# Turning the intermediate spectrum with VectorE in 32x32 squares instead of TensorE transposes, in a long-convolution kernel

## The chip, the cores and the metric

The kernel runs on one core of a Trainium2 chip. A core has five engines, each with its own queue of instructions that it works off in order: TensorE (PE in the profile, with its weight loads shown apart as PEld), VectorE (DVE), ScalarE (ACT), GpSimd (POOL) and SyncE (SP), which here does nothing but issue DMA transfers. They meet only at semaphores. TensorE writes its results to PSUM, eight banks of 128 partitions by 512 float32, from which VectorE and ScalarE copy them to SBUF. The metric is the device time of one execution in microseconds (us). A span runs from the first to the last instruction of the profiled execution.

## The reference

For a sequence u of 2048 steps by 512 channels:

```python
xn = layernorm(x)                                    # over the 512 channels
K[d, l] = Re(sum_n C[d,n] * dt*B[d,n] * exp(dt*A[d,n]*l))   # 128 complex modes
s = irfft(rfft(xn, 4096) * rfft(K, 4096))[:2048] + xn * Dskip   # causal convolution per channel
g = silu(gelu(xn @ w1 + b1) @ w2 + b2)               # 512 -> 1792 -> 512
return x + s * g
```

All is float32. The part that is changed is the way back of the convolution (the inverse transform), the product with g, and the sum with x.

## The kernel before

The program has two stages. The first, up to about 394 us of the trace, makes g (the two matrix products, each operand split in a high and a low part), the kernels K, and the normalised input; g goes to DRAM scratch tiles `gd`, K to `kgd`. The second stage, about which all of this document is, does the convolution. The two overlap for about 12 us.

**Blocks.** The convolution works in four blocks `b` of 128 channels. The 2048 steps are split as 32 by 64 (`N1 = 32`, `N2 = 64`), and the long transform is done as two short ones, both as matrix products with constant tables: `first_dft` over 32 (F below) and `second_dft` over 64 (S). The way back has a transform over 64 (`back_dft`, B), a turn that brings the other axis into the partitions (`swing`, w) and a transform over 32 (`last_dft`, L). F is done for u and for K, in two halves of channels each: four groups `(u, h)` a block, one block ahead.

**Slots.** S is cut into eight slots `g` of a block (`slot(b, g)`, L1020; main loop L1122). The program is written in the order in which each engine is to work it off, without a planner in this stage. Each slot begins with S on TensorE (L883: 32 small products with 64-row, 64-column tiles, each of them two instructions). ScalarE copies half of the result to SBUF (`spectrum`, tile `uh`, L891), and VectorE forms the two products with it (`product`, L900). After two slots `combine` (L909 to L912) makes the real and imaginary parts from sums and differences of these, in four instructions on 64 partitions, into the tile `Y`. Its rows 0 to 63 hold the real, 64 to 127 the imaginary parts.

Even slots also hold an F group for block b+1 (`first_dft`, L864; the results are copied by ScalarE, `first_out`, L870). Odd slots hold a B (`back_dft`, L918: two calls of four 128x128 products with the constant table `tcn`; `back_out`, L930, copies each call's bank into `Z`). The turn of block b-1 is in slots 3 and 5 (`swings`): 32 TensorE transposes (L936) of 128x128, each four copied out by ScalarE into tiles `bs` (`swing_out`, L944). The last transform of b-1 (`last_dft`, L975) is in slots 5 and 7: 64-row, 32-column tiles with the table `gc`, 512 columns. `last_out` multiplies the result with g on VectorE (L982) and adds x on GpSimd (L983); `store` (L992) sends it out.

**Loads and stores of the end.** For each block b-1, g and x come in four quarters (`tail_load`, L961 and L964, in slots 0, 1, 2 and 5, six transfers each), and the results leave in 16 transfers, all on SP's queue. Tiles `gb` and `xb` have three buffers each.

**PSUM.** Four of the eight banks belong to S (`ri`: two buffers of two banks). The other four serve F, B, w and L in turn (`bank`, L803: two pools, "c" and "a", of two buffers each, taken alternately). F takes all four, since its four channel groups run side by side; a call of B takes one.

**The last block** has no F. Its slots take the turn of block 2 in slots 2 to 5 and half of L of block 2 in slot 4; the other half follows after the slots. Then comes the end (L1125 to L1144): the last B, four dummy transposes (L1135), the turn in four quarters, L, products, sums and stores. Its loads go through GpSimd's queue in slots 1 to 4. Two of its quarters are done in another form (`rows_out`, L1006 to L1014), with a second table `gc2`.

Of the kernel before, what the change touches and what calls it, by code (L numbers as in the profile page):

```python
# [11 lines left out]
F32 = mybir.dt.float32  # L12
# [8 lines left out]
P = 128  # L21
L, D, NS, F = 2048, 512, 128, 1792
G = D // P
# [107 lines left out]
def _shape_constants():  # L131
# [4 lines left out]
    cg = np.zeros((2, N1, 2, 3, N1))  # L136
    for hh in range(2):
        for c, v in enumerate((np.cos(a).T, -np.sin(a).T)):
            cg[hh, :, c, 0] = v
            cg[hh, :, c, 1:].reshape(N1, N1, 2)[:, :, hh] = v  # L140
    cg = cg.reshape(P, 3 * N1)
# [14 lines left out]
    ct = ct.reshape(P, N1, 2, 2, 2, 16).transpose(0, 1, 4, 5, 3, 2)  # L156
# [16 lines left out]
def kernel(  # L173
# [7 lines left out]
    x_t = u[0].rearrange("(n h j t a q) d -> t h a j n q d", n=N1, h=2, j=2, t=2, a=2)  # L181
    o_l = out[0].rearrange("(r j q) d -> j r q d", j=2, q=NQ)
    o_t = out[0].rearrange("(n h j t a q) d -> t h a j n q d", n=N1, h=2, j=2, t=2, a=2)
    x_l = u[0].rearrange("(r j q) d -> j r q d", j=2, q=NQ)

# [5 lines left out]
    gd = [dram.tile([P, NQ * P], F32, name=f"gd{b}") for b in range(NB)]  # L191
# [251 lines left out]
    def z_store(t):  # L443
        zi = fin[t]
        for b in range(NB):
            (GP if t == NTB - 1 else SY).dma_start(gd[b].rearrange("p (q m) -> p q m", m=P)[:, t * TB:(t + 1) * TB, :], zi[:, :, b * P:(b + 1) * P])
# [341 lines left out]
    def open_mid():  # L788
        SB["pm"] = pm = opened(p2, "pm", "right")
        SB["ps"] = opened(pz, "psm", "left", bufs=2, space=PSUM)  # L790
        SB["tcn"] = pm.tile([P, N1, P], F32, name="tcn")
        SB["gc"] = pm.tile([P, N1], F32, name="gc")
# [109 lines left out]
    def combine(b, j, c, eng, js=slice(0, 4)):  # L902
        t, w = sm[b, j]
        if (b, j) not in yy:
            yy[b, j] = SB["pm"].tile([P, 4, 2, P], F32, tag="Y", name=f"Y_{b}_{j}", bufs=2)
        Y = yy[b, j].rearrange("p j a (r x) -> p a r j x", r=2)
        for ka in range(2):
            r = slice(ka * 64, ka * 64 + 64)
            if c == 0:  # L909
                eng.tensor_sub(Y[0:64, ka, :, js], t[r, 0, :, js], w[r, 1, :, js])  # L910
            else:
                eng.tensor_add(Y[64:128, ka, :, js], t[r, 1, :, js], w[r, 0, :, js])  # L912

    def back_dft(b, j, h):
        Y = yy[b, j].rearrange("p j a m -> p (j a) m")
        p = bank(f"sa{b}_{j}_{h}")
        for e in range(4):
            PE.matmul(p[:, e, :], Y[:, 4 * h + e, :], SB["tcn"][:, 8 * j + 4 * h + e, :], start=True, stop=True)  # L918
        yy[b, j, h] = p

    def back_out(b, j, h, engs=(A,)):
        if (b, "Z") not in yy:
            yy[b, "Z"] = SB["pm"].tile([P, 32, 2, N1, 2], F32, tag="Z", name=f"Z{b}", bufs=2)
        k = 8 * j + 4 * h
        src = yy.pop((b, j, h)).rearrange("p k (x h c) -> p x h k c", h=2, c=2)
        dst = yy[b, "Z"][:, :, :, k:k + 4, :]
        w = 4 // len(engs)
        for i, eng in enumerate(engs):
            n = slice(w * i, w * i + w)
            eng.copy(dst[:, :, :, n], src[:, :, :, n]) if eng is A else eng.tensor_copy(dst[:, :, :, n], src[:, :, :, n])  # L930

    def swing(b, q4, jj, wide=None):
        Z = yy[b, "Z"].rearrange("p (j r t q) h k c -> p j r t q (h k c)", j=2, r=2, t=2)
        p = bank(f"w{b}_{q4}_{jj}") if wide is None else wide[:, jj]
        for e in range(4):
            PE.transpose(p[:, e, :], Z[:, jj, q4 // 2, q4 % 2, e, :], ident)  # L936
        yy[b, q4, jj] = p

    def swing_out(b, q4, jj, eng):
        if jj == 0:  # L940
            yy[b, q4, "s"] = SB["pm"].tile([P, 2, 4, P], F32, tag="bs", name=f"bs{b}_{q4}", bufs=3)
        dst = yy[b, q4, "s"][:, jj].rearrange("p e (x r) -> p e r x", r=2)
        src = yy.pop((b, q4, jj)).rearrange("p e (r x) -> p e r x", r=2)
        A.copy(dst, src) if eng is A else V.tensor_copy(dst, src)  # L944

    gx = {}
    gc2 = dsk.rearrange("p b d -> p (b d)")[:, :2 * N1]

    def tail_load(b, i, q=SY, rows=False):
        cs = slice(b * P, (b + 1) * P)  # L950
        t = gx.pop((b, i, "t"), None) or new_tail(b, i)
        gx[b, i] = t
        if rows:
            n = slice(4 * i, 4 * i + 4)
            q.dma_start(t[0], gd[b].rearrange("p (q m) -> p q m", m=P)[:, n])
            for j in range(2):
                q.dma_start(t[1][j * 64:(j + 1) * 64], x_l[j, :, n, cs])
            return
        for a in range(2):
            r = slice(a * 64, (a + 1) * 64)  # L960
            q.dma_start(t[0][r], gd[b].rearrange("(j n h) (t a q m) -> t h a j n q m", n=N1, h=2, t=2, a=2, m=P)[i // 2, i % 2, a])  # L961
            for j in range(2):
# [212 lines left out]
```

## Time and profile before

| | |
|---|---|
| Three timed runs | 560.02, 560.35 (median), 561.1 us |
| Span of the profiled execution | 558.0 us |
| Around the span (start and end of the execution), median less span | 2.35 us |
| TensorE clock granted, mean | 0.998 |
| First S of block 0, 1, 2, 3 starts at | 405.9, 436.5, 473.1, 509.6 us |
| Last S ends | about 536.6 us |
| VectorE, last sum of the last block begins | 552.62 us |

The time of the profiled execution itself is not listed apart from the three; its span is what the rows below belong to. A row of the groups (by line) has the line, engine, operation, output and inputs with shapes, the count, then the busy time, the mean of one in ns, the idle time of the engine before them and what ended it. A row of the chain of waits or of the timeline has the start in us, the length in us, the engine and the line, with the number of instructions behind the x.

### The profile page before, as it was taken

How to read it: one execution, taken by the hardware profiler on the slowest of the kernel's cores; microseconds unless marked ns; L12 is line 12 of the kernel's file. 1: busy time of each engine (PE TensorE's matmuls, PEld its weight loads, DVE VectorE, ACT ScalarE, POOL GpSimd, SP SyncE). 2: the span in 40 equal slices, each digit the busy share in tenths (PEclk: the TensorE clock that was granted, in tenths of full speed). 3: DMA queues.
4: the chain of work that ended last, by engine and by line, in shares of the span. 5: the costliest groups of instructions: out<-in, count | busy, mean ns of one | idle time of the engine just before them, and what ended most of it. 6: DMA issues, size and time to landing. Idle time of an engine off the chain costs nothing.

```text
span 558.0 us, 17143 instructions
## 1 busy us (share of the span) xinstructions
PE 540.2 (97%) x7179; PEld 432.1 (77%) x7179; DVE 454.2 (81%) x697; ACT 407.8 (73%) x602; POOL 296.3 (53%) x403
## 2 busy tenths in 40 slices
PE   8899999999999999999999999999999999999995
PEld 7567777777777777767777777777889998988872
DVE  6899999999997799988988969877357657767874
ACT  3589997977598999668989798995355565564542
POOL 5639585776966769857718747540320305014323
PEclk9999999999999999999999999999999999999999
DMA  8959337267468392426167049205965583615945
GB/s 188 288 161 311 84 96 210 61 210 228 135 189 269 133 295 81 143 75 192 57 188 219 21 114 186 61 11 181 365 245 79 140 128 95 191 46 127 197 120 113
DMA packets 108345, 86.92 MB, mean 156 GB/s; under 512 B 44294, under 2 KB 87562, under 8 KB 108268
## 3 DMA queue, kind: packets, MB, share of 16 engines
q1 hardware_dynamic: 97584, 65.37, 43.8%
q0 software_dynamic: 9568, 19.93, 12.1%
q8 instruction: 56, 0.92, 0.7%
q10 hardware_dynamic: 1116, 0.53, 0.4%
q14 instruction: 21, 0.17, 0.1%
HBM read 52.25 MB, written 33.55 MB: 154 GB/s over the span
## 4 chain that ended last, share of the span: by engine, by line
PE 68%; DVE 16%; issue 6%; DMA 5%; SPq 2%; ACT 1%; POOL 1%; DVEq 0%; POOLq 0%
PE z L295 8%; PE z L296 7%; PE z L297 7%; PE f L256 7%; PE f L258 7%; PE f L257 7%; PE s L883 6%; PE kg L656 5%; PE s L864 4%; PE sa L918 3%; DMA w2s<-in_B_w_dram 2%; PE ph L595 2%; PE w L936 2%; DVE e L641 2%; DVE hl L282 2%
## 5 line engine op out<-in xcount | busy, mean ns | idle before, releaser
L618 POOL TENSOR_TENSOR mm<-mm,rc 128x32 f32<-128x32 f32 (+4 forms) x150 | 110.7, 738 | 11.8
L295 PE MATMUL z<-w2h,hh 128*128 128x512 f32 x224 | 97.9, 437 | 0.0
L256 PE MATMUL f<-xh,w1h 128*128 128x512 f32 x220 | 92.0, 418 | 0.5 <-ACT hf L270 0.5
L297 PE MATMUL z<-w2h,hl 128*128 128x512 f32 x224 | 88.5, 395 | 0.9 <-DVE hl L282 0.9
L296 PE MATMUL z<-w2l,hh 128*128 128x512 f32 x224 | 88.7, 396 | 0.0
L258 PE MATMUL f<-xh,w1l 128*128 128x512 f32 x220 | 86.9, 395 | 1.5 <-DVE w1l L241 1.5
L257 PE MATMUL f<-xl,w1h 128*128 128x512 f32 x220 | 86.7, 394 | 0.0
L883 PE MATMUL s<-X,mc 64*64 64x128 f32 x2048 | 63.5, 272 | 0.9 <-issue 0.9
L900 DVE TENSOR_TENSOR t<-s,uh 128x512 f32<-128x512 f32 x64 | 41.1, 685 | 25.9 <-ACT uh L891 25.6
L883 PEld LDWEIGHTS s<-X,mc 64*64 64x64 f32 x2048 | 56.0, 133 | 4.8 <-issue 2.7
L641 DVE TENSOR_TENSOR e<-mm,ra 128x1024 f32<-128x1024 f32 x32 | 47.8, 1495 | 4.7 <-POOL mm L618 3.2
L297 PEld LDWEIGHTS z<-w2h,hl 128*128 128x128 f32 x224 | 42.1, 188 | 11.7 <-DVE hl L282 1.8
L258 PEld LDWEIGHTS f<-xh,w1l 128*128 128x128 f32 x220 | 41.3, 188 | 11.9 <-DVE w1l L241 2.1
L615 POOL COPY mm<-rc 128x32 f32<-128x32 f32 x30 | 15.4, 512 | 65.4 <-DVE e L648 49.0
L256 PEld LDWEIGHTS f<-xh,w1h 128*128 128x128 f32 x220 | 41.5, 189 | 10.3 <-ACT hf L270 1.2
L282 DVE TENSOR_TENSOR hl<-hf,hh 128x512 fp32r<-128x512 f32 x56 | 46.7, 838 | 3.4 <-ACT hh L276 3.3
L295 PEld LDWEIGHTS z<-w2h,hh 128*128 128x128 f32 x224 | 42.5, 190 | 9.0
L609 DVE SCALAR_TENSOR_TENSOR ra<-ra,ph 128x512 f32<-128x512 f32 x64 | 43.6, 681 | 6.9 <-ACT ra L603 6.0
L296 PEld LDWEIGHTS z<-w2l,hh 128*128 128x128 f32 x224 | 42.3, 189 | 7.9
L257 PEld LDWEIGHTS f<-xl,w1h 128*128 128x128 f32 x220 | 41.4, 188 | 8.9
L870 ACT COPY X<-s 128x512 f32<-128x512 f32 x56 | 28.9, 598 | 25.6 <-PE s L864 25.6
L645 DVE TENSOR_TENSOR e<-mm,ra 128x1024 f32<-128x1024 f32 x32 | 45.6, 1425 | 0.0
(185 smaller groups left out, 1146.2 us busy)
## 6 DMA issues: line engine op xcount, KB each, us to landing
x<-in_A_u_dram SPq DMA_DIRECT2D x16, 256.0 KB
xs<-x SPq DMA_DIRECT2D x16, 256.0 KB
xt_h<-xh POOLq DMA_DIRECT2D x4, 1024.0 KB, 5.4
xt_l<-xl POOLq DMA_DIRECT2D x4, 1024.0 KB, 7.3
kgd<-ko SPq DMA_DIRECT2D x32, 128.0 KB
za<-zo SPq DMA_DIRECT2D x4, 1024.0 KB
xh<-xt_h POOLq DMA_DIRECT2D x4, 1024.0 KB, 6.8
xl<-xt_l POOLq DMA_DIRECT2D x4, 1024.0 KB, 10.1
```

What stands on the lines that cost most here:

```text
L256: PE.matmul(p, wh[:, k, :], xh[:, k, :], start=(k == 0), stop=False)
L257: PE.matmul(p, wh[:, k, :], xl[:, k, :], start=False, stop=False)
L258: PE.matmul(p, wl[:, k, :], xh[:, k, :], start=False, stop=(k == KD - 1))
L282: V.tensor_sub(hl, hf, hh)
L295: PE.matmul(z, hh[:, s], wh, start=(f0 == 0 and not rows), stop=False)
L296: PE.matmul(z, hh[:, s], wl, start=False, stop=False)
L297: PE.matmul(z, hl[:, s], wh, start=False, stop=(f0 == FA - 1))
L609: V.scalar_tensor_tensor(ra[:, 0, c], ra[:, 1, c], MAGIC, p, op0=ALU.subtract, op1=ALU.subtract)
L618: GP.tensor_mul(mv[:, :, 0:3:2, w:2 * w], mv[:, :, 0:3:2, 0:w], rc[:, 2 + 2 * i:4 + 2 * i, :].rearrange("p j c -> p c j").unsqueeze(3).to_ ...
L641: V.tensor_mul(e1, m1.unsqueeze(1).to_broadcast([P, 2, CH, N1]), ra[:, :, :, :N1])
L645: V.tensor_mul(e2[:, :, :, :H], m2[:, :, :H].unsqueeze(1).to_broadcast([P, 2, CH, H]), ra[:, :, :, dn])
L883: PE.matmul(p[ka * 64:(ka + 1) * 64, r, o, :, jj], mc[h, k, ((0, 2), (1, 0))[c][o], :], xf[b][h, c, :, k, :], start=(c == 0), stop=(c == 1 ...
```

## The change

The turn goes from TensorE to VectorE, and what stands around it is laid out anew.

- `combine` writes `Y` as two planes (real, imaginary) with 128 rows: two instructions on 128 partitions in place of four on 64. So that both halves of the rows hold what belongs together, S takes its frequencies in another order.
- `back_dft` contracts 64 rows at a time: rows 0 to 63 go to one bank, 64 to 127 to another, real and imaginary part one after the other into the same place. 16 calls in place of 8, each with half of the rows.
- `turn` transposes 32x32 squares on VectorE, from `Z` (now two halves of a block) into a tile `T`: four instructions of 128x1024 a block. `swing`, `swing_out`, the dummy transposes and `rows_out` go.
- `last_dft` is one group a block: 32 calls with 32 rows and 32 columns of the array (16 tiles), 512 columns, two calls adding up in a place.
- The order of the slots: F groups in slots 0, 2, 5 and 6; B in slots 1, 3, 5 and 7; the second turn of block b-1 in slot 2, the first turn of block b in slot 6; L, with four products, in slot 4; four sums on GpSimd in slots 5 and 6, then one store of four transfers.
- `tail_load` fetches a whole block with eight transfers, in slots 0 and 1, into one buffer `gb` and one `xb`. The scratch `gd` is laid out by time tile.
- In the last block, the first turn is in slot 5, half of the last B in slot 7; the end has the other half, two turns, L in two parts, and products, sums and stores in two halves of the rows.

```diff
     def second_dft(b, g):
...
-                            k, h = 4 * g + 2 * jj + ka, slice(r * 64, (r + 1) * 64)
+                            k, h = 8 * (g // 2) + 4 * ka + 2 * (g % 2) + jj, slice(r * 64, (r + 1) * 64)
...
     def combine(b, j, c, eng, js=slice(0, 4)):
...
-        for ka in range(2):
-            r = slice(ka * 64, ka * 64 + 64)
-            if c == 0:
-                eng.tensor_sub(Y[0:64, ka, :, js], t[r, 0, :, js], w[r, 1, :, js])
+        Y = yy[b, j][:, c].rearrange("p j (r x) -> p r j x", r=2)
+        if c == 0:
+            eng.tensor_sub(Y[:, :, js], t[:, 0, :, js], w[:, 1, :, js])
+        else:
+            eng.tensor_add(Y[:, :, js], t[:, 1, :, js], w[:, 0, :, js])
+
+    def back_dft(b, j, es=range(4)):
+        Y = yy[b, j]
+        if (b, j, "p") not in yy:
+            yy[b, j, "p"] = [bank(f"sa{b}_{j}_{a}") for a in range(2)]
+        ps = yy[b, j, "p"]
+        for e in es:
+            for c in range(2):
+                for a in range(2):
+                    r = slice(64 * a, 64 * a + 64)
+                    PE.matmul(ps[a][:, e, :], Y[r, c, e, :], SB["tcn"][r, 8 * j + 2 * e + c, :],
+                              start=(c == 0), stop=(c == 1), skip_group_check=True)
+
+    def back_out(b, j, eng=A, m=slice(0, N2)):
...
+        for a, p in enumerate(yy[b, j, "p"]):
+            k = 8 * (j % 2) + 4 * a
+            dst = yy[b, "Z", j // 2][:, m, :, k:k + 4]
+            src = p.rearrange("p k (c n) -> p n c k", c=2)[:, m]
+            A.copy(dst, src) if eng is A else eng.tensor_copy(dst, src)
+
+    def turn(b, h, i, n=2):
+        if i == 0:
+            yy[b, "T", h] = SB["pm"].tile([P, N2, N1], F32, tag="T", name=f"T{b}_{h}", bufs=2)
+        m = slice(i * N2 // n, (i + 1) * N2 // n)
+        V.transpose(yy[b, "T", h][:, m].rearrange("p n c -> p (n c)"), yy[b, "Z", h][:, m].rearrange("p n c k -> p (n c k)"))
...
+    def last_dft(b, hs=(0, 1), gs=range(G), wide=False):
...
+        py = gx[b, "y"]
+        for h in hs:
+            T = yy[b, "T", h]
+            for g in gs:
+                for q in range(G):
+                    r = slice(q * N1, (q + 1) * N1)
+                    PE.matmul(py[q][g * N1:(g + 1) * N1], SB["gc"][r, h], T[r, 16 * g:16 * g + 16].rearrange("p n c -> p (n c)"),
+                              start=(h == 0), stop=(h == 1), skip_group_check=True)
+
+    def last_gate(b):
+        g = gx[b][0].rearrange("p n (a c r) -> p r a n c", a=2, r=2)
+        for q in range(G):
+            d = g[:, q // 2, q % 2]
+            V.tensor_mul(d, gx[b, "y"][q].rearrange("p (n c) -> p n c", c=N1), d)
...
+    ahead = {0: (0, 0), 2: (0, 1), 5: (1, 0), 6: (1, 1)}
 
     def slot(b, g):
...
+        back = {1: (b - 1, 3), 3: (b, 0), 5: (b, 1), 6 if last else 7: (b, 2)}.get(g)
...
+        u = None if last else ahead.get(g)
         second_dft(b, g)
...
+        if back:
+            back_dft(*back)
+        if u:
+            first_dft(b + 1, *u, range(G))
+        if b and g == 4:
+            last_dft(b - 1)
+        if last and g == 7:
+            back_dft(b, 3, (0, 1))
         spectrum(b, g)
...
+        if back:
+            back_out(*back)
+        if u:
+            first_out(b + 1, *u)
         product(b, g)
...
+        if b and g == 2:
+            turn(b - 1, 1, 0)
+            turn(b - 1, 1, 1)
+        if g == (5 if last else 6):
+            turn(b, 0, 0)
+            turn(b, 0, 1)
+        if b and g == 4:
+            last_gate(b - 1)
+        if b and g in (5, 6):
+            for k in range(2 * g - 10, 2 * g - 8):
+                n = slice(4 * k, 4 * k + 4)
+                last_add(b - 1, n)
+            if g == 6:
+                store(b - 1)
+        if b and g < 2:
+            tail_load(b - 1, SY, g)
+        if last and g == 1:
+            big = SB["pf"].tile([P, 2, NQ, P], F32, tag="X0", name="last")
+            tail_load(b, GP, 2, (big[:, 0], big[:, 1]))
...
         b = NB - 1
...
+        last_dft(b, (0,), wide=True)
+        back_dft(b, 3, (2, 3))
+        for i, eng in enumerate((A, V)):
+            back_out(b, 3, eng, slice(32 * i, 32 * i + 32))
+        for i in range(2):
+            turn(b, 1, i)
+            last_dft(b, (1,), range(2 * i, 2 * i + 2))
+        lo, hi = slice(0, 8), slice(8, NQ)
+        last_gate_wide(b, lo)
+        last_add(b, slice(0, 4), V)
+        last_add(b, slice(4, 8), GP)
+        store(b, lo, (SY, A, SY, A))
+        last_gate_wide(b, hi)
+        last_add(b, slice(8, 13), V)
+        last_add(b, slice(13, NQ), GP)
+        store(b, hi, (SY, A, SY, A))
```

More of the change, by code (lines that the diff above doesn't have):

```diff
@@ L135, in _shape_constants @@
     cf = np.tile(np.stack([np.cos(a), -np.sin(a)], 1), (G, 1, 1))
[L136 to L141, printed above, removed]
+    cg = np.stack([np.cos(a).T, -np.sin(a).T]).reshape(2, 2, N1 // 2, N1)
+    cg = np.tile(cg.transpose(0, 2, 1, 3).reshape(N1, 2 * N1), (G, 1))
     n2 = np.arange(N2)[:, None]
@@ L932, in swing @@
[L932 to L962, printed above, removed]
-                r = slice(a * 64 + j * N1, a * 64 + (j + 1) * N1)
-                q.dma_start(t[1][r], x_t[i // 2, i % 2, a, j, :, :, cs])
@@ new lines, in slot @@
+        if u:
[4 more added lines that the diff above has]
+            back_dft(b, 3, (0, 1))
+        spectrum(b, g)
+        if back:
+            back_out(*back)
+        if u:
+            first_out(b + 1, *u)
+        product(b, g)
+        if last and g > 5:
+            for c in range(2):
+                combine(b, i, c, V, slice(2 * g - 12, 2 * g - 10))
+        elif g % 2:
+            for c in range(2):
+                combine(b, i, c, V)
```

191 lines of the change are left out of this document (45 added, 146 removed).

## The prediction, made before the changed kernel was run

> **What bounds the kernel now.** I first read the page's totals, then the busy time by stretches cut at the first S of each block, then the chain of waits inside a block.
>
> ```profile
> span 558.0 us, 17143 instructions
> PE 540.2 (97%) x7179; PEld 432.1 (77%) x7179; DVE 454.2 (81%) x697; ACT 407.8 (73%) x602; POOL 296.3 (53%) x403
> ...
> PE 68%; DVE 16%; issue 6%; DMA 5%; SPq 2%; ACT 1%; POOL 1%; DVEq 0%; POOLq 0%
> ...
> 405.96:436.54 30.58, 29.73 (x817) 27.40 (x816) 19.24 (x30) 16.96 (x31) 7.10 (x8) 1.00 0.51 129
> 436.54:473.13 36.59, 36.59 (x897) 32.70 (x896) 23.55 (x36) 21.66 (x40) 7.92 (x8) 1.00 0.67 133
> 473.13:509.63 36.50, 36.50 (x898) 32.60 (x897) 24.76 (x36) 21.65 (x40) 5.91 (x7) 1.00 0.44 119
> 509.63:536.62 26.99, 26.00 (x609) 23.11 (x609) 23.04 (x35) 12.56 (x22) 14.19 (x22) 1.00 0.83 185
> 536.62:558.00 21.38, 13.65 (x112) 8.79 (x108) 12.28 (x22) 6.21 (x11) 5.03 (x4) 0.95 0.42 92
> ```
>
> The columns of the last five rows are length, then PE, PEld, DVE, ACT and POOL busy. TensorE is busy all of blocks 1 and 2 while VectorE is at 24 of 36.5 us and ScalarE at 22: there, a TensorE instruction removed is time removed, and VectorE has 12 us of room. In the last 21 us no engine is full; that stretch is a chain of dependences. The change touches nothing before 405.96.
>
> A slot's price is read from the chain of waits of block 1, which runs on TensorE without a break (start, length, line, instructions):
>
> ```profile
> 446.26 1.94 PE s L864 x64
> 448.20 2.01 PE s L883 x62
> 450.21 1.98 PE sa L918 x16
> 452.19 1.75 PE w L936 x16
> 453.94 1.91 PE s L883 x64
> 455.85 1.94 PE s L864 x64
> 457.79 1.91 PE s L883 x64
> 459.70 1.02 PE y L975 x16
> ```
>
> So S is 1.91, F 1.94, B 1.98, half a turn 1.75 and half of L 1.02. A block costs 8 S + 4 F + 4 B + 2 turns + 2 L = 15.28 + 7.76 + 7.92 + 3.50 + 2.04 = 36.50, the length of block 2 exactly.
>
> **The change, part by part.**
>
> *Turn off TensorE.* Blocks 1 and 2 lose 3.50 each. In the last block the 32 transposes go from the slots, and 32 more with four dummies from the end.
>
> *B.* 16 calls are 32 instructions (two each, as now 8 calls give 16) with 64 rows. S puts four 64x64 tiles side by side: 128 columns of B take 1.98 / 16 = 124 ns, S takes 1.91 / 64 = 30 ns an instruction, a quarter. F shows that tiles that differ only in rows overlap too: 128 wide, 1.94 / 64 = 30 ns. B needs two side by side: 32 x 124 / 2 = 1.98, as before. The other end is 3.96, if the halves queue. I take 1.98, the row of S and F being the nearer.
>
> *L.* 64 instructions of 512 columns on 16 tiles; now 16 on 8 tiles take 1.02, so one round of all tiles takes 0.51 and four rounds 2.04, as the two halves cost now. The low end is 64 starts at F's 30 ns, 1.94; the high end 4.08, if 16 tiles give no more than 8. I take 2.04.
>
> [...]
>
> *VectorE and ScalarE.* These rows price them (busy, mean ns):
>
> ```profile
> L641 DVE TENSOR_TENSOR e<-mm,ra 128x1024 f32<-128x1024 f32 x32 | 47.8, 1495 | 4.7 <-POOL mm L618 3.2 <-ACT ra L629 0.7 <-issue 0.4
> L900 DVE TENSOR_TENSOR t<-s,uh 128x512 f32<-128x512 f32 x64 | 41.1, 685 | 25.9 <-ACT uh L891 25.6
> L912 DVE TENSOR_TENSOR Y<-t,t 64x512 f32<-64x512 f32 x30 | 23.5, 784 | 0.7
> L910 DVE TENSOR_TENSOR Y<-t,t 64x512 f32<-64x512 f32 x30 | 20.6, 685 | 0.7
> L982 DVE TENSOR_TENSOR gb<-y,gb 128x512 f32<-128x512 f32 x10 | 6.7, 688 | 12.8 <-issue 6.0 <-PE y L975 5.9 <-DMA gb<-gd 0.9
> L944 DVE COPY bs<-w 128x512 f32<-128x512 f32 x2 | 1.3, 686 | 0.7 <-PE w L936 0.7
> L930 DVE COPY Z<-sa 128x256 f32<-128x256 f32 x1 | 0.4, 423 | 1.4 <-ACT Z L930 1.4
> 463.39 1.96 DVE L912 TENSOR_TENSOR Y<-t,t 64x512 f32<-64x512 f32 x2
> L944 ACT COPY bs<-w 128x512 f32<-128x512 f32 x30 | 17.0, 657 | 4.6 <-PE w L936 4.6
> ```
>
> A combine goes from four of 0.73 to two of 0.7: 2.94 to 1.4, saving 1.5 us a pair of slots. A turn instruction is new. Copies of 256 and 512 columns, 423 and 686 ns, give 160 ns and 1.03 ns a column: 1.2 us for 1024. The ends: 0.69, if a 1024-column turn took what a 512-column copy does, and 3.0, twice the 1.5 us of L641, the row of its size. I take 1.2, a copy being the nearest kind. VectorE's block is then 8 products of 1.3 (10.4), four combines (5.6), four turns (4.8), four gates of 0.69 (2.8): 23.6 of 34 us. TensorE hides it; the cover is gone where these instructions lie ahead of something TensorE waits for, which is so in the last block only. ScalarE loses 8 copies of 0.657 a block.
>
> [...]
>
> *A new wait in slot 5.* This the trace of before doesn't show, and I work it out from the banks. B and F share four banks. B's two banks now both fill until its last instruction (rows 0 to 63 in one, 64 to 127 in the other), while now the first call's bank is copied out during the second call. In slot 5 of blocks 0 to 2 an F, which takes all four banks, stands right behind B. Its third and fourth channel group need B's banks. These rows give the price:
>
> ```profile
> 448.22 2.05 ACT L870 COPY X<-s 128x512 f32<-128x512 f32 x4 [1.26 <-PE s L864]
> 450.30 0.59 ACT L891 COPY uh<-s 128x512 f32<-128x512 f32 x1
> 451.34 0.59 ACT L930 COPY Z<-sa 128x512 f32<-128x512 f32 x1 [0.45 <-PE sa L918]
> 452.23 0.59 ACT L930 COPY Z<-sa 128x512 f32<-128x512 f32 x1 [0.31 <-PE sa L918]
> ```
>
> A copy is 0.59, four in a row 2.05, so the next begins 0.49 later. Both copies after B's end: 0.05 to start, 0.59 + 0.49, 0.05 to wake TensorE, about 1.2 us; F's groups are interleaved, so its first instructions save nothing: F is 1.15 late. In slot 6 F follows with only an S (1.91) for the four X copies (0.09 + 2.05): 0.2 late. Together 1.35 a block, in three blocks 4.0. The other end is nothing, if the banks come free sooner than I read. I take 1.35, because the order in the program forces it. What is behind the waiting F on TensorE is S of slot 6; VectorE and ScalarE have room and follow it. S itself waits for nothing: its buffer is free when the product two slots before is done, 2.0 us after that S, and between lie 3.8 or more.
>
> *Queues.* SP issues 8 + 4 transfers a block in place of 24 + 16. GpSimd's queue for the last block issues 8 in place of 18 of about 0.6 us. GpSimd's sums stay four a block. With single buffers, the loads of a block wait for the sums and stores of the one before: stores leave in slot 6, the loads in slots 0 and 1, and they are needed in slot 4, some 15 us on; landings of 4 to 7 us, by the rows of the last block's loads on GpSimd's queue, are covered.
>
> ```profile
> last<-gd POOLq DMA_DIRECT2D x4, 128.0 KB, 4.3
> ...
> last<-in_A_u_dram POOLq DMA_DIRECT2D x4, 128.0 KB, 6.9
> ...
> L964 POOL DMA_DIRECT2D last<-in_A_u_dram x8 | 4.5, 565 | 0.0
> ```
>
> Without that cover it is what the old order shows in slot 0 of the last block:
>
> ```profile
> 505.98 3.10 DMA gb<-gd
> ...
> 509.20 0.69 DVE gb L982
> ...
> 514.06 0.70 DVE Y L910
> 514.80 1.83 PE sa L918 x14
> ```
>
> There g came late, the products with it held up S's products and `Y`, and TensorE lost about 1 us. That goes.
>
> *The last block,* from its first S as zero, by hand from the same rows. TensorE runs S, S+B, S, S+B, S+L to 15.5. The gates of block 2 (VectorE, 16.1 to 18.8, behind a product that the turn of slot 2 had put off) hold two banks until 17.45, when B of slot 5 starts; it ends 19.45. VectorE then has a product, a combine and two turns to 24.5, with 0.65 for the combine running beside GpSimd's sums (the row at 463.39: 1.96 for two, otherwise 1.39). B of slot 6 waits for that combine and ends at 24.2; the last S at 26.1. Products of slots 6 and 7 end at 25.8 and 28.1, the combine at 29.0. L's first part ends at 29.15, the last half of B at 30.15. Then nothing is hidden: two copies 0.9, turn 1.2, turn 1.2 with L's third quarter beside it, L's fourth 1.1, to 34.5; two gates 1.35 and a sum of 0.7, two more gates 1.3, a sum of 640 columns 0.85, to 38.8; and the stores. What a store costs from the start of the last queue is shown by the old end:
>
> ```profile
> 552.62 0.69 DVE L1012 TENSOR_TENSOR last<-last 128x512 f32<-128x512 f32 x1
> 553.34 0.68 SPq L1014 DMA_DIRECT2D out_dram<-last  x1
> ```
>
> From 553.34 to 558.0 are 4.66, and now two transfers stand in each queue, 0.65 more: 44.2. Now it is 558.0 - 509.63 = 48.4.
>
> *The sum.* Block 0: 30.58 + 1.35 = 31.9. Blocks 1 and 2: 15.28 + 7.76 + 7.92 + 2.04 + 1.35 = 34.35 each. 405.96 + 31.9 + 2 x 34.35 + 44.2 = 550.8 us of span. The median of the three runs is 560.35, 2.35 over the span; 550.8 + 2.35 = **553.1**, 1.3% under it.
>
> **The rivals.**
>
> *No bank wait.* For it: "issue" and copies leave some room; against it: L870 never starts before F's end (1.26 idle ahead of it). It gives 553.1 - 4.0 = 549.
>
> *Dear turns: slower.* One mechanism: an instruction of `turn` takes over 2.1 us. With 2.4, L of slot 4 waits 0.9, the gates and the B behind them 2.3, the turns of slot 5 hold the product that slot 7 needs, 5.3 by the end of the slots, two exposed turns 2.4 more, 1.3 in blocks 1 and 2: about 9 us, so 562. That is 7.5 us for each us of a turn; 7.2 us of gain are used up at 1.2 + 0.95 = 2.15. At 3.0 it is 566.6. For it: L912 shows VectorE disturbed, and the operation is unseen. Against: every row of one input lies near 1 ns a column.
>
> *L doesn't get 16 tiles.* At 4.08 it costs 2.04 in blocks 1 and 2, about 1.6 in slot 4 of the last block, 2 at the end: 7.7, so 561, no change. [...]
>
> *B's halves queue.* 1.98 for each of 15 B and more at the end: 30 us, 583. F and S speak against it.
>
> **How the numbers follow.** Chances: forecast 0.57; no bank wait 0.14; dear turns 0.14 (0.05 below break-even, 0.03 near it, 0.06 beyond); L short of 16 tiles 0.10 (half of it near 557, half near 561); B's halves 0.05. A measurement of this kernel tells about 0.2%, 1.1 us, from no change. Faster: 0.57 + 0.14 + 0.05 + 0.05 = 0.81; same 0.03 + 0.05 = 0.08; slower 0.06 + 0.05 = 0.11. The forecast's own range is 550.5 to 556, for an end that is worked out by hand. [...]
>
> **What would show it.** No w on TensorE in the slots; B at 1.98 for 32 and L at 2.04 for 64 instructions; a hole of about 1.15 us ahead of or inside F in slot 5 of blocks 0 to 2, ended by Z of ScalarE, and first S's at 437.9, 472.2 and 506.6; four turns a block of 1.2; no wait for `gb`; last sum 39 us after the last block's first S. It is wrong if S waits for products (VectorE in front of TensorE), if TensorE waits for `T`, or if B or L run at half their pace.

## The result, and the profile after

The changed kernel takes 586.88 us (median of four runs, 583.04 to 598.95) against 560.18 us before: a ratio of 1.0444, interval 1.0406 to 1.0482. The highest of the four was disturbed and is not in the ratio. The forecast was 553.1 us, with 548 to 559 as the range of 8 in 10. The profiled execution took 586.59 us, 584.6 of them span. In the line numbers of the changed kernel, S is L878, F L859, B L916 (`sa`), L is L964 (`y`), the turn L932, the combine L903 and L905, the gate with g L971, and the sums on GpSimd L981.

The page's totals and the granted clock in 40 slices of the span (in tenths, 9 is 90% or more):

```profile
span 584.6 us, 17461 instructions
PE 539.3 (92%) x7439; PEld 429.5 (73%) x7439; DVE 448.7 (77%) x678; ACT 390.0 (67%) x572; POOL 294.3 (50%) x393
PEclk9999999999999999999999999999899789799797
```

The same stretches as before, cut at each block's first S (length, then PE, PEld, DVE, ACT, POOL busy, granted clock, DMA share, GB/s):

```profile
405.72:440.29 34.57, 31.86 (x866) 29.42 (x865) 17.23 (x26) 16.22 (x30) 7.12 (x8) 0.95 0.46 115
440.29:485.12 44.83, 37.96 (x963) 33.68 (x961) 24.62 (x33) 17.09 (x32) 10.20 (x9) 0.89 0.64 120
485.12:528.20 43.08, 37.35 (x963) 32.76 (x961) 24.69 (x33) 17.14 (x32) 7.96 (x10) 0.92 0.49 100
528.20:584.60 56.40, 35.12 (x802) 26.93 (x800) 32.04 (x47) 10.70 (x20) 12.85 (x12) 0.88 0.58 114
```

Two things are new. TensorE was busy for all of blocks 1 and 2 before; now it stands still for 44.83 - 37.96 = 6.9 us of block 1 and 5.7 us of block 2. And the clock, 1.00 in these blocks before, is 0.89 and 0.92 (0.95 and 0.88 in the other two), so that TensorE is busy 37.96 us in block 1 where the forecast had 34.35 in all.

The groups of instructions from 440 us on (count, busy us, mean ns, idle before and what ended it) show that VectorE is not what held it up. It stood idle 50.8 us for ScalarE's copies of S, and S on TensorE stood idle 13.2 us, none of it put down to VectorE:

```profile
L878 PE MATMUL s<-X,mc 64*64 64x128 f32 x1536 | 53.3, 290 | 13.2 <-issue 13.2
L895 DVE TENSOR_TENSOR t<-s,uh 128x512 f32<-128x512 f32 x49 | 31.5, 684 | 50.8 <-ACT uh L886 50.6
L932 DVE STREAM_TRANSPOSE T<-Z 128x1024 f32<-128x1024 f32 x14 | 16.5, 1218 | 0.0
```

The turn costs 1.218 us, forecast at 1.2. TensorE's timeline in block 1 has the prices and the holes side by side (start, length, line, instructions; in brackets the idle time before and what ended it):

```profile
446.05 1.39 PE L916 MATMUL sa<-tcn,Y 64*128 64x128 f32 x20
449.29 0.94 PE L916 MATMUL sa<-tcn,Y 64*128 64x128 f32 x12 [1.86 <-issue]
450.16 1.98 PE L878 MATMUL s<-X,mc 64*64 64x128 f32 x64
452.06 1.77 PE L859 MATMUL s<-fc,in 32*128 32x64 f32 x51
458.48 1.12 PE L859 MATMUL s<-fc,in 32*128 32x64 f32 x13 [4.65 <-issue]
459.53 3.09 PE L878 MATMUL s<-X,mc 64*64 64x128 f32 x64
462.55 2.06 PE L916 MATMUL sa<-tcn,Y 64*128 64x128 f32 x32
464.54 1.98 PE L878 MATMUL s<-X,mc 64*64 64x128 f32 x64
466.45 2.35 PE L964 MATMUL y<-T,gc 32*32 32x512 f32 x64
468.73 1.98 PE L878 MATMUL s<-X,mc 64*64 64x128 f32 x64
470.63 2.06 PE L916 MATMUL sa<-tcn,Y 64*128 64x128 f32 x32
472.62 0.44 PE L859 MATMUL s<-fc,in 32*128 32x64 f32 x4
473.36 2.65 PE L859 MATMUL s<-fc,in 32*128 32x64 f32 x60 [0.30 <-ACT Z L926]
475.94 1.34 PE L878 MATMUL s<-X,mc 64*64 64x128 f32 x20
```

From start to start, B takes 464.54 - 462.55 = 1.99 and L 468.73 - 466.45 = 2.28. The bank wait in slot 5 is there, ended by `Z`. But the two large holes, 1.86 and 4.65 us, stand *inside* a B and inside an F: the group's first instructions have run, so its operands and banks are there, and the next one of the same group does not come. The releaser is "issue", that is, nothing that the profile shows. Four more, two in block 2 and two in block 3, stand inside an S:

```profile
496.46 0.67 PE L878 MATMUL s<-X,mc 64*64 64x128 f32 x16 [2.06 <-issue]
503.85 1.22 PE L878 MATMUL s<-X,mc 64*64 64x128 f32 x17 [3.31 <-issue]
538.90 2.62 PE L878 MATMUL s<-X,mc 64*64 64x128 f32 x84 [3.54 <-issue]
548.42 3.25 PE L878 MATMUL s<-X,mc 64*64 64x128 f32 x53 [4.34 <-issue]
```

Together the six are 19.8 us. After the second hole of block 1 TensorE is slow: the S at 459.53 takes 3.09 in place of 1.98. The trace's clock record is at one half from 455.0 for 6.8 us, and so it is from 502.8 and from 547.2 for 6.8 us, beginning each time in the second hole of a block, and from 475.5 for 3.4 us, behind the bank wait. The first hole of each block had no such stretch behind it, nor had the bank waits of blocks 0 and 2.

The DMA view of three stretches in block 1, from 446 to 449.3, to 453.8 and to 458.5 us, shows what else was going on (packets, MB, share):

```profile
q1 hardware_dynamic: 417, 0.76, 96.8%
q8 instruction: 1, 0.02, 2.3%
...
q1 hardware_dynamic: 1600, 0.88, 120.5%
...
q1 hardware_dynamic: 580, 0.28, 40.9%
q8 instruction: 1, 0.02, 1.6%
```

q1 is SP's queue, here with the eight loads of g and x of 256 KB each, issued in slots 0 and 1; its share is of the time of all 16 DMA engines, and as the times of its packets are added up it can pass 100%. q8, which the view calls an instruction queue, has 16 KB in a packet. Its counts fit TensorE's instructions: 58 packets with the 7439 products and as many weight loads of this program, 56 with the 7179 of the old one, so about 256 of these instructions, or 128 products, to each. While q1 fills the engines, q8's packets come late: they start at 446.5 and 455.8, 9.3 us apart, where before in the same place they came at 442.6, 447.0 and 451.9. TensorE goes on 2.8 and 2.7 us after the start of these two, and after the other four holes 2.6 to 2.9 us after the start of one. And the two holes of a block are one packet apart: between them TensorE runs 12 + 64 + 51 products in block 1, 16 + 64 + 47 in block 2 and 84 + 32 + 11 in block 3, each time 127. So the holes stand where, by these counts, one packet ends and the next has not arrived.

Block 0, 2.7 us over the forecast, lost them in another way. The timeline of VectorE, and that of TensorE, at the S of slot 2:

```profile
415.14 1.89 DVE L895 TENSOR_TENSOR t<-s,uh 128x512 f32<-128x512 f32 x3 [4.73 <-DMA gd<-zi]
...
411.00 3.46 PE L878 MATMUL s<-X,mc 64*64 64x128 f32 x64
415.93 1.98 PE L878 MATMUL s<-X,mc 64*64 64x128 f32 x64 [1.48 <-ACT uh L886]
```

The second product of slot 0 waits for a *store*, `gd<-zi`: the last tile of g is still being written out when VectorE wants to put a product there. (The S of 411.00 is slow for another reason: the clock is at half from 410.7 for 3.4 us. That began ahead of the wait, behind a hole of 0.87 us put down to issue.) In the old kernel the tiles `gb` and `xb` were taken in slot 0 and lay on that place; now they are taken in block 1, and the product tile has moved down onto it.

### The profile page after: what moved, and what is told of

Its sections match the earlier page's. It is cut to its first block, busy times and chain, and to the rows that moved or that the text cites. A ratio compares the mean times of both kernels' runs of the same rounds, so it can differ in the third digit from the quotient of the medians.

```text
span 584.6 us, 17461 instructions
## 1 busy us (share of the span) xinstructions
PE 539.3 (92%) x7439; PEld 429.5 (73%) x7439; DVE 448.7 (77%) x678; ACT 390.0 (67%) x572; POOL 294.3 (50%) x393
## 4 chain that ended last, share of the span: by engine, by line
PE 72%; DVE 16%; issue 6%; DMA 3%; ACT 2%; POOL 0%; POOLq 0%; SPq 0%; DVEq 0%
PE s L878 10%; PE z L290 7%; PE z L291 7%; PE z L292 7%; PE f L251 7%; PE f L253 6%; PE f L252 6%; PE s L859 6%; PE sa L916 5%; PE kg L651 5%; PE ph L590 2%; DMA w2s<-in_B_w_dram 2%; DVE e L636 2%; PE y L964 2%; DVE hl L277 2%
## 5 line engine op out<-in xcount | busy, mean ns | idle before, releaser
L878 PE MATMUL s<-X,mc 64*64 64x128 f32 x2048 | 70.8, 290 | 15.6 <-issue 14.1
L878 PEld LDWEIGHTS s<-X,mc 64*64 64x64 f32 x2048 | 62.3, 144 | 22.5 <-issue 16.5
L981 POOL TENSOR_TENSOR xb<-gb,xb 128x512 f32<-128x512 f32 x12 | 17.6, 1497 | 72.5 <-DVE gb L971 72.5
L886 ACT COPY uh<-s 128x512 f32<-128x512 f32 x32 | 18.7, 586 | 52.8 <-issue 25.2
L636 DVE TENSOR_TENSOR e<-mm,ra 128x1024 f32<-128x1024 f32 x32 | 46.6, 1456 | 3.7 <-POOL mm L613 2.3
```

The costliest lines, as they stand in the source:

```text
L636: V.tensor_mul(e1, m1.unsqueeze(1).to_broadcast([P, 2, CH, N1]), ra[:, :, :, :N1])
L878: PE.matmul(p[ka * 64:(ka + 1) * 64, r, o, :, jj], mc[h, k, ((0, 2), (1, 0))[c][o], :], xf[b][h, c, :, k, :], start=(c == 0), stop=(c == 1 ...
```

## The experiments

The theory after this profile: (T) the loads, drawn together into eight transfers of 256 KB in two slots, fill the DMA engines, so that TensorE's instruction packets come late, and each hole costs again by a halved clock; (P) the placement in block 0 is a smaller cost of its own. The rivals: the changed TensorE program needs its packets faster whatever the loads do; or any burst of DMA does it.

**Loads left out, loads spread, a burst in the old kernel.** In the first of three kernels, the loads for blocks 1 to 3 go, so that the later blocks work on the tiles of block 0:

```diff
-        if b and g < 2:
-            tail_load(b - 1, SY, g)
+        if b == 1 and g < 2:
+            tail_load(0, SY, g)
...
```

> The changed kernel with the loads of g and x for blocks 1, 2 and 3 left out (those of block 0, which come in block 1's slots 0 and 1, stay as they are, and the later blocks work on the same tiles). T: block 1 keeps its holes and its length of about 44.8 us, blocks 2 and 3 lose them (block 2 about 34.5 us from first S to first S, was 43.1), the clock is halved once and not later; 563 to 568 us. R1 and R2: blocks 2 and 3 stay above 40 and 52 us, time above 580 us.

570.79 us, ratio 1.0167 (1.0136 to 1.0198). TensorE's timeline in block 1, where block 0's loads are still made:

```profile
451.70 0.94 PE L916 MATMUL sa<-tcn,Y 64*128 64x128 f32 x12 [1.86 <-issue]
460.90 1.12 PE L859 MATMUL s<-fc,in 32*128 32x64 f32 x13 [4.65 <-issue]
```

These are the holes of the changed kernel, to the hundredth and at the same instructions. In blocks 2 and 3, with the same TensorE program and without loads, there is no hole put down to issue above 0.25 us, and block 2 is 34.5 us long in place of 43.1, as expected. That speaks for T and against a program that needs its packets faster by itself. The time is 2.8 us over the range that was expected: block 0 and block 1, which keep their costs, are 36.4 and 44.8 us long, and block 3 is 47.2.

In the second, one piece of g is loaded in each of slots 0 to 3 and one of x in each of slots 1 to 4 (the last block's own in its slots 4 to 7), each held there by a one-column write of VectorE into its place:

```diff
-        if b and g < 2:
-            tail_load(b - 1, SY, g)
+        if b and g < 4:
+            tail_piece(b - 1, g, 0, SY)
+        if b and 0 < g < 5:
+            tail_piece(b - 1, g - 1, 1, SY)
...
```

> The changed kernel with the same 16 loads of g and x a block pair, but no longer in two bursts: one 256 KB transfer of g in each of slots 0 to 3 and one of x in each of slots 1 to 4, each held back by a one-column fill that VectorE does after that slot's products; the loads of the last block go out in its slots 4 to 7. Theory T (the burst of loads holds up the 16 KB packets in which TensorE's instructions arrive, TensorE runs dry, and a hole of some us is followed by a halved clock): the holes inside instruction groups of blocks 1 to 3 (19.8 us together) shrink to under 3 us together, the mean clock goes from 0.971 to over 0.99, and the time is 555 to 563 us. Rival R1 (the new program is denser in TensorE instructions, 960 pairs a block for 896, and starves with any loads) and rival R2 (the 16-tile products bring the clock down by themselves): 580 us and more, holes or clock as before.

575.2 us, ratio 1.024 (1.0195 to 1.0285). The holes went as expected: in blocks 1 to 3 only 0.42 and 0.48 us are put down to issue. The one of 0.42 stands at the place of the 1.86; at the place of the 4.65 there is none. The time did not come down as expected: the last piece of g now comes late (2.5 us of TensorE behind `gb` in block 3), and in block 0 the product waits for the store, as VectorE's timeline shows:

```profile
415.18 1.89 DVE L895 TENSOR_TENSOR t<-s,uh 128x512 f32<-128x512 f32 x3 [5.80 <-DMA gd<-zi]
```

A hole of 3.72 us ahead of S goes with it, and the S, F and S behind the hole take 3.69 us each in place of 1.98, 2.01 and 1.98. So pace cured the holes, and P is no small cost here.

In the third, the old kernel gets eight transfers more of 256 KB in slot 1 of blocks 1 to 3, from DRAM to DRAM:

```diff
...
+        if b and g == 1:
+            for k in range(4):
+                SY.dma_start(sc[0][k], u[0][k * P:(k + 1) * P, :])
+            for k in range(4):
+                SY.dma_start(sc[1][k], u[0][k * 512:(k + 1) * 512, :P])
```

> The kernel before, with eight transfers of 256 KB from DRAM to a DRAM scratch added on SP's queue in slot 1 of blocks 1, 2 and 3; nothing reads the scratch. T: holes of 1 to 5 us inside instruction groups on TensorE, with no engine named as their cause, in slots 1 to 4 of these blocks, although the program of TensorE is the old, less dense one; the clock is halved after the longer ones; 568 to 590 us. R1 and R2: no such holes; at most a later g, 560 to 566 us.

563.14 us, ratio 1.0061 (1.0032 to 1.0089), and no hole put down to issue in blocks 1 to 3. The expectation of T fell: a burst as such is not enough. One row of TensorE's timeline is of use all the same:

```profile
477.93 3.42 PE L866 MATMUL s<-fc,in 32*128 32x64 f32 x62 [1.86 <-DVE gb L984]
```

Here TensorE stood for 1.86 us, a wait that the trace puts down to VectorE's product with g, and F takes 3.42 in place of 2.01 and the S behind it 3.69 in place of 1.98: nearly twice as long, as B did in the half-clock stretch of the changed kernel from 502.8 (3.78 in place of 2.06). So idle time of another cause had slow products behind it too.

**What sort of burst.** The kernel without loads got such DRAM to DRAM transfers in slots 0 and 1 of blocks 2 and 3:

```diff
...
+        if b > 1 and g == 0:
+            for k in range(4):
+                SY.dma_start(sc[0][k], u0[k * P:(k + 1) * P, :])
+        if b > 1 and g == 1:
+            for k in range(4):
+                SY.dma_start(sc[1][k], u0[k * 512:(k + 1) * 512, :P])
...
```

> The kernel that leaves out the loads of blocks 1, 2 and 3, with eight transfers of 256 KB from DRAM to a DRAM scratch in their place in slots 0 and 1 of blocks 2 and 3; nothing reads the scratch. If any backlog on SP's queue starves TensorE when it runs this program, holes of 2 to 5 us come back in blocks 2 and 3 and the time is 578 to 590 us. If it must be loads that write to SBUF, or if DRAM to DRAM leaves no backlog, it stays at the 571 us of the kernel without those loads.

573.34 us, ratio 1.0226 (1.0191 to 1.0261). In block 2, TensorE's timeline:

```profile
495.86 0.67 PE L881 MATMUL s<-X,mc 64*64 64x128 f32 x16 [0.69 <-issue]
```

That is the place at which the changed kernel has 2.06; of the others put down to issue in blocks 2 and 3 one is 0.29, and the rest are gone. As many bytes from DRAM to DRAM did much less here than the loads into SBUF. Two kernels, with the tiles in their old place (below), load one half only in blocks 2 and 3, g alone or x alone (in slot 1, in the same manner):

```diff
...
+        if b > 1 and g == 0:
+            gx[b - 1] = (SB["pm"].tile([P, NQ, P], F32, tag="gb", name=f"gb{b - 1}"), gx[b - 2][1])
+            tail_load(b - 1, SY, 0)
...
```

> The changed kernel with both tiles in their old place; the loads of x for blocks 1 to 3, and of g for block 3, are left out (the products and sums read what stands there). In block 1 both loads remain. If g's loads hold up the instruction packets: in blocks 2 and 3 a hole of about 2 us after slot 0's loads, none after slot 1. If it takes the whole 2 MB: no hole above 0.7 us there.

> The same with x loaded and g left out in blocks 2 and 3: if x's loads hold up the packets, a hole of 3 to 5 us about 8 us after slot 1's issues; if it takes the whole 2 MB, none above 0.7 us there.

568.65 and 575.35 us, one execution each, so that the two times can't be weighed against each other. TensorE's timeline with g alone:

```profile
491.52 0.67 PE L878 MATMUL s<-X,mc 64*64 64x128 f32 x16 [2.06 <-issue]
```

and with x alone:

```profile
495.49 1.07 PE L878 MATMUL s<-X,mc 64*64 64x128 f32 x16 [2.06 <-issue]
```

Each half gives the first hole of block 2, at the same instruction and as long as in the changed kernel; neither gives the second, 3.31 us there. In block 3, where the last block's own loads are left out of both, no hole put down to issue is over 0.4. So it is neither g nor x by itself: in block 2 a megabyte of either gave one hole, and two megabytes gave two. In block 3 a megabyte gave none, so the amount isn't all of it. The 2 us expected for g came, the 3 to 5 for x didn't.

**Placement and size of the pieces.** One kernel takes the first `gb` and `xb` in slot 0 again, as the old one did, with a pad behind; the second cuts the changed kernel's loads into 128 KB of g and 64 KB of x, by turns; the third does both.

```diff
+        if (b, g) == (0, 0):
+            gx[0] = tuple(SB["pm"].tile([P, NQ, P], F32, tag=m, name=f"{m}0") for m in ("gb", "xb"))
+        if (b, g) == (0, 1):
+            SB["pm"].tile([P, 2016], F32, tag="pad", name="pad")
```

```diff
...
+        for k in range(4) if part == 2 else (2 * part, 2 * part + 1):
+            c = slice(k * N1, (k + 1) * N1)
+            for h in range(2):
+                q.dma_start(g[c].rearrange("n (t q) m -> n t (q m)", t=NTB)[:, 2 * h:2 * h + 2],
+                            gd[b].rearrange("t (j n i) m -> i j n t m", j=2, i=2)[k // 2, k % 2, :, 2 * h:2 * h + 2])
+                for e in range(2 * h, 2 * h + 2):
+                    q.dma_start(x[c, 4 * e:4 * e + 4], x_c[k, :, 4 * e:4 * e + 4, cs])
```

> The changed kernel with only the place of its tiles moved: the two tiles for g and x are taken in slot 0 of block 0 and 8 KB are left empty, so that these tiles, not the product tile t1, lie where the first stage's last part of g (zi) still waits to be stored. Theory P: VectorE's first product into t1 waited 4.7 us for the landing of that store, S of slot 2 began at 415.9 instead of 413.0 and the clock was halved for 3.4 us; all of this goes, S of slot 2 begins at about 413, and the time falls by 3.5 to 6 us to 581 to 583.5 us, with the holes of blocks 1 to 3 as they are. Rival: the wait is for the table load that comes at the same time; then nothing changes, 587 us.

> The changed kernel with the same loads in the same slots of the same queue, cut into pieces of the old size: 8 of 128 KB for g and 16 of 64 KB for x a block, alternating, in place of 8 of 256 KB. Theory T (SP hands out 256 KB in about 0.5 us, faster than the transfers run, and TensorE's instruction packets stand behind the backlog): SP's 0.45 us an issue now paces the loads; the holes of blocks 1 to 3 shrink from 19.8 us to under 5 us, and the time to 560 to 570 us. Rival V (the volume of 2 MB in few slots does it, at any pace): holes over 12 us, time over 578 us.

> The small pieces and the moved tiles together. T and P: 555 to 566 us, the sum of both gains; no clock halved before the end of the last block. V: over 574 us.

Placement alone: 582.7 us, ratio 1.0399 (1.034 to 1.0457), and in TensorE's timeline the S of slots 1 and 2 run without a break:

```profile
410.68 3.88 PE L878 MATMUL s<-X,mc 64*64 64x128 f32 x128
```

P holds, at 586.88 - 582.7 = 4.2 us; block 0 is 30.8 us long in place of 34.6. That is more than the wait alone: the stretch at half clock from 410.7 is gone as well. Small pieces alone: 575.31 (1.025 to 1.0306), a miss: a hole of 2.63 in block 0 stayed, with an S and an F of 3.69 each behind it, and two of 1.33 and 2.98 in block 3. Both: 565.78 (1.0078 to 1.013), at the upper end of what was expected; but products ran at about half speed twice ahead of the end, behind the bank wait of block 0 (S 3.24 in place of 1.98) and in the last block (B 3.22, S 3.01), which had not been expected. The holes in blocks 1 and 2 are down to 0.76 or less. What is left is in the last block, in VectorE's and TensorE's timelines:

```profile
533.12 2.48 DVE L969 TENSOR_TENSOR gb<-y,gb 128x512 f32<-128x512 f32 x4 [6.78 <-DMA xb<-in_A_u_dram]
...
529.07 1.75 PE L878 MATMUL s<-X,mc 64*64 64x128 f32 x53 [1.88 <-issue]
533.86 3.22 PE L916 MATMUL sa<-tcn,Y 64*128 64x128 f32 x32 [3.04 <-DVE gb L969]
```

There SP's loads for block 2 and GpSimd's for block 3 run at the same time, 4 MB in two slots: TensorE stands 1.88 us inside an S, and VectorE's gate stands 6.8 us for the loads; B, whose banks the gate reads, stands for the gate.

**Mending what is left.** Three versions, each built on the one before. First, all of g ahead of x, and the last block's loads in its slots 4 to 7, a piece of each a slot:

```diff
...
-            tail_load(b, GP, 2, (big[:, 0], big[:, 1]))
...
+            tail_piece(b, g - 4, 0, GP)
+            tail_piece(b, g - 4, 1, GP)
```

> The changed kernel with both tiles in their old place, the loads cut into 128 KB of g (all of them first, slot 0) and 64 KB of x (slot 1), and the last block's loads on GpSimd's queue moved to its slots 4 to 7, one piece each a slot. Theory (transfers hold up TensorE's instruction packets, and holes are followed by half a clock): no hole put down to issue above 1 us in blocks 1 to 3, g in time in the last block, clock halved only after bank waits and at the end: 556 to 561 us, ratio 0.993 to 1.002. Rival (something else in the change costs, and the transfers only shift it): it stays at the 565.8 us of the small pieces in the old place.

563.37 us, ratio 1.0062 (1.0036 to 1.0089): no hole put down to issue above 1 us, but 2 us more than expected. The second copies one of the two banks of slot 5's B on VectorE, in blocks 0 to 2:

```diff
-            A.copy(dst, src) if eng is A else eng.tensor_copy(dst, src)
+            A.copy(dst, src) if (eng, a) != (V, 1) and m != slice(32, 64) else V.tensor_copy(dst, src)
...
-            back_out(*back)
+            back_out(*back, V if g == 5 and not last else A)
```

> The one before, and in slot 5 of blocks 0 to 2 the second of the two Z copies on VectorE, beside the first on ScalarE. Theory: the bank wait in front of F in slot 5 goes from 1.2 us to about 0.7, 1.5 us in three blocks, and the windows of half a clock that follow such waits go where they were: 1.5 to 4 us under the run without it, 553 to 558. Rival (the copy on VectorE puts off products, and S waits for them): equal or slower.

561.96 us, ratio 1.0046 (1.0021 to 1.007), 1.4 us under the one before, with intervals that overlap, and 4 us over what was expected. What went with it can be seen in the products behind the bank waits. Behind the bank wait of block 0, TensorE's timeline without this edit has

```profile
430.01 3.40 PE L878 MATMUL s<-X,mc 64*64 64x128 f32 x64
```

and with it

```profile
428.96 1.98 PE L878 MATMUL s<-X,mc 64*64 64x128 f32 x64
```

The S behind each of the three bank waits of 1.2 to 1.4 us took 3.40, 3.44 and 3.64, and behind those of 0.9 us that took their place 1.98 each. Part of that can be chance: in the ten kernels that keep the longer wait, 14 of its 26 cases had an S of 3.24 to 3.64 behind them. The changed kernel has one of them among its three, where the clock record is at half for 3.4 us. The rest of the time was in the last block, where `Y` kept B waiting for 1.55 and 3.03 us. VectorE's timeline there, and GpSimd's:

```profile
526.97 0.69 DVE L903 TENSOR_TENSOR Y<-t,t 128x512 f32<-128x512 f32 x1
527.57 3.10 DVE L905 TENSOR_TENSOR Y<-t,t 128x512 f32<-128x512 f32 x1
534.43 2.93 DVE L903 TENSOR_TENSOR Y<-t,t 128x256 f32<-128x256 f32 x1
...
527.62 2.50 POOL L993 TENSOR_TENSOR xb<-gb,xb 128x512 f32<-128x512 f32 x2
534.58 2.49 POOL L993 TENSOR_TENSOR xb<-gb,xb 128x512 f32<-128x512 f32 x2
```

A combine takes 0.69, or 0.41 for 256 columns. Beside GpSimd's two sums it takes 3.10 and 2.93: its own time and nearly all of theirs. The third version runs these four sums on VectorE after the last combine, and puts the last block's loads on SP's queue in slots 2 to 5:

```diff
...
-        if b and g in (5, 6):
+        if b and g in (5, 6) and not last:
...
+        if last and g == 7:
+            for k in range(4):
+                last_add(b - 1, slice(4 * k, 4 * k + 4), V)
+            store(b - 1)
...
```

> The version with the Z copy on VectorE, changed in the last block alone: block 2's four sums run on VectorE behind the combine of slot 7 (where it stood idle for 2.8 us) in place of GpSimd in slots 5 and 6, and the last block's loads are on SP's queue in slots 2 to 5. Theory (a combine that runs beside GpSimd's sums takes 3 us in place of 0.7 or 0.4, and S and B wait for it): combines at 0.7 and 0.4, the two waits for Y of 1.55 and 3.03 gone, the last block 4 to 5 us shorter: 554.1 us of span, 555 to 559 us, ratio 0.991 to 0.997. Rival (the combines wait for something else, or SP's loads beside the slots give a new hole): the waits for Y stay or a hole of 2 to 3 us comes, and the time stays at 560 to 562.

558.67 us, ratio 0.9966 (0.9931 to 1.0001): as expected. (The kernel changes both things at once, so the run doesn't part them.) VectorE's timeline of the same combines, of slot 5 and slot 6:

```profile
532.14 0.68 DVE L905 TENSOR_TENSOR Y<-t,t 128x512 f32<-128x512 f32 x1
536.58 0.42 DVE L903 TENSOR_TENSOR Y<-t,t 128x256 f32<-128x256 f32 x1
```

and the stretches by block:

```profile
407.57:439.81 32.24, 30.48 (x866) 28.16 (x865) 17.74 (x27) 15.79 (x29) 7.11 (x8) 1.00 0.48 123
439.81:475.99 36.18, 34.59 (x962) 30.64 (x961) 24.46 (x34) 16.66 (x31) 9.80 (x9) 1.00 0.68 148
475.99:511.47 35.48, 34.36 (x962) 30.25 (x961) 24.53 (x34) 16.66 (x31) 6.17 (x7) 1.00 0.51 123
511.47:556.60 45.13, 31.47 (x802) 25.00 (x800) 33.55 (x59) 10.70 (x20) 3.36 (x2) 0.92 0.65 142
```

The clock is full in blocks 0 to 2. This is the change with most of its side effects gone, and about 0.3% under the old kernel, at the edge of what can be told apart. In its profile the first S lies 1.6 us later than in the old one's, for which the runs show no cause; from there on it is 149.0 us against 152.0.

## Why the prediction was wrong

| block | forecast | changed kernel | last version |
|---|---|---|---|
| 0 | 31.9 | 34.57 | 32.24 |
| 1 | 34.35 | 44.83 | 36.18 |
| 2 | 34.35 | 43.08 | 35.48 |
| 3, to the end | 44.2 | 56.40 | 45.13 |
| sum | 144.8 | 178.9 | 149.0 |

*The step that failed* is the paragraph on the queues. It counted SP's transfers, found fewer, took landings of 4 to 7 us as covered by the 15 us to their use, and charged nothing: the forecast set this term at zero. The cover is real for the data, but data was not all that the DMA engines brought: the packets of q8 went over the same 16 engines (0.7% of their time in the changed kernel), and with 2 MB of loads into SBUF in two slots they came late, 9.3 us apart in block 1. The six holes are 19.8 us. TensorE's busy time adds to it: it is 11.4 us more in the changed kernel (the four rows add up to 142.3) than in the last version (130.9), for the same products, because of the halved clock (five stretches before the end, 27.3 us, in which TensorE was busy for 21.6). The idle time is 18.5 us more (178.9 - 142.3 against 149.0 - 130.9). Together that is the difference of 29.9 us between the versions; the placement in block 0 and the waits of the last block are in it too.

*A second step wasn't there:* the forecast followed the tiles' waits, but not where they lie. About 4 us in block 0 come with a product tile that moved onto a tile still being stored.

*The steps that held.* B: 1.98 forecast, 1.99 seen. The turn: 1.2, and 1.218. The bank wait in slot 5 was to make F 1.15 late; it made it 1.21 late in blocks 0 and 2. In slot 6 F was 0.1 late, forecast at 0.2. In slot 5 of block 1, from 472.62 to the next S it took 475.94 - 472.62 = 3.32 in place of 1.94, 1.38 more, of which the end ran at half the clock. The combine: 0.7, and 0.69 when undisturbed.

*Mis-sized.* L was 2.28 against 2.04. It costs 3 x 0.24 us in the slots. No run shows the term behind the 557 us to which the chances give half of the case that L falls short; what the changed kernel showed is an L of 2.28. The combine beside GpSimd's sums was put at 0.65 us more for a pair. In the changed kernel a single one takes 1.69 to 1.76, 1.0 more, and in the version with the Z copy on VectorE 2.4 and 2.5 more. The changed kernel mostly hides this: from 440 us on, TensorE waits 0.5 us there for `Y`, against 1.55 and 3.03 in that version.

*The rivals.* None came. A dear turn, the slower side of the forecast, is ruled out by 1.218; the slower result came from a term that had been set at zero. The last version, 149.0 against 144.8 from the first S, suggests that the sum of the other terms was about 4 us too low, though that version is another kernel, with a shorter bank wait. What it has over the forecast is L, small holes of 0.3 to 1.0 us put down to issue (3.5 in all, of which the old kernel had 0.85), and 0.9 in the last block. Even so mended, the change wins a third of a per cent, not 1.3%: of the 3.50 us taken off TensorE in blocks 1 and 2, 36.18 and 35.48 against 36.59 and 36.50 leave 0.4 and 1.0.

*What stays open.* Why the same bytes from DRAM to DRAM, or in the old kernel's smaller pieces, held up TensorE less. Why a megabyte gave a hole in block 2 and none in block 3. No run here loads 2 MB into SBUF in the old kernel.

## What to carry to other kernels

Loads that landed long before they were needed weren't free here: 2 MB in two slots went with 19.8 us of holes in three blocks. Where TensorE runs long unrolled code, count the megabytes that are issued at once, spread them over the slots in small pieces, and look for holes put down to "issue" in the middle of a group. Price every idle time on TensorE again for the clock: here 14 of 26 bank waits of 1.1 to 1.4 us had an S of 3.24 to 3.64 us behind them, in place of 1.98. And when a tile is taken at another time, look at what lay on its place.

## What the runs showed of the hardware

*TensorE's instructions came late.* In the kernels with the changed program the holes put down to issue in blocks 1 to 3 stand at the same places of it or whole packets apart (127 products between the two holes of a block in the changed kernel), and whether and how long they are goes with the loads: after the first 51 products of the same F in block 1, 4.65 or 4.92 us with the burst of 2 MB, 0.3 or less with small pieces or one piece a slot. In the changed kernel TensorE went on 2.6 to 2.9 us after the start of a packet of 16 KB on q8, at all six of them.

*The clock fell after short idle times.* In the changed kernel a stretch at half clock, of 6.8 us, begins inside the second hole of blocks 1 to 3 (4.65, 3.31 and 4.34 us), and none follows the first holes of 1.86, 2.06 and 3.54. In the old one, with the burst, an F of 3.42 us in place of 2.01 and an S of 3.69 in place of 1.98 follow a wait of 1.86; with x alone, the 16 products behind a hole of 2.06 take 1.07 in place of 0.67, and the F behind them 3.69. Bank waits of 1.1 to 1.4 us had an S of 3.24 to 3.64 behind them in 14 of 26 cases, those of 0.9 us in none of 6. So in these runs the length of an idle time did not tell by itself whether the clock fell. The stretches at half clock in the changed kernel begin at 410.67, 455.05, 475.53, 502.83 and 547.21, which is 13, 6, 8 and 13 times 3.41 us apart, and last 3.41 or 6.83 us.

*Combines on VectorE took longer beside sums on GpSimd.* In the version with the Z copy, the combine of 3.10 us, 0.69 + 2.41, ended 0.55 us after two sums of 2.50 together, although it started with them. In the changed kernel five of the six combines of 512 columns that lay beside sums took 1.69 to 1.76 us and one 0.69.
